# Raw queries and keys in three buffers and loaded three quads ahead, scalings one step sooner, a smaller descriptor scratch, and two small moves around the first expert block

## Chip, core and metric

One core of a Trainium2 chip runs the whole program. The metric is the device time of one execution in microseconds (us), as a median over runs. Engine names are those of the profile: PE (TensorE matmuls), PEld (its weight loads), DVE (VectorE), ACT (ScalarE), POOL (GpSimd), SP (SyncE, which here mainly issues DMAs).

## What is computed

Attention with capped scores for 8 batches, 12 heads, 448 positions and head size 64, and then a mixture of 8 experts with one expert per token over the 3584 resulting rows of 768:

```python
scores = (q @ k.T) / sqrt(64)
scores = cap * tanh(scores / cap)
attn   = softmax(scores)                  # over the last axis
x      = (attn @ v), heads side by side   # [3584, 768]
e      = argmax(x @ w_gate), gate = softmax(x @ w_gate)[e]
out    = gate * (relu(x @ w1[e]) @ w2[e]) # w1: [8, 768, 1024], w2: [8, 1024, 768]
```

All inputs and the output are float32.

## The kernel before, in words

**Attention.** The work is cut into 24 quads (four heads of one batch each, so three quads make a batch), each quad into 7 tiles of 64 keys, and the 168 tiles are taken two at a time in 84 steps. The order on every engine is the order in which the code is written. A step `k` issues, in this order: `scores` and `tanh` of its two tiles (PE, ACT), `expo(k - 1)` (ACT), the products with the values, `values(k)`, of tiles some three steps back (PE), the copies `outp` of a finished quad out of PSUM (DVE), the tasks put down for the places "pe1" and "v0", `adds(k - 2)` (DVE, the sums of the softmax), and the tasks of the places "v1" and "v". A table filled by `at(step, place, function)` says which task stands where.

**Queries.** The raw queries and keys of a quad come by DMA into a tile `qk` (`load(mq, 0)`, the values into `vr` by `load(mq, 1)`), issued from SP. The pool `raw` holds two `qk` tiles, so the load of quad n + 2 waits until PE has read the last scores of quad n. DVE scales the queries in place (`scale_q`, L266), so the scores of a quad wait for its scaling, and the scaling for its DMA. For even quads the scaling stands at place "v0", ahead of `adds`; for odd ones at "v1".

**Routing.** When a batch is finished, its rows go through the gate: `sums`, `rec_v`, `logits`, `log_v` (DVE, its last row is L415, which writes `lr`), then `rec_p` and `log_p` (PE; `log_p`, L427, reads `lr`), `route_v`, `place_p` and so on, spread over the following steps. PE takes `log_p` in its place in the step, ahead of the next step's scores.

**Experts.** Tokens are gathered into blocks of up to 448 rows with indirect DMAs issued from POOL (L742), which have their descriptors in a scratch at the start of each SBUF partition. A first block, number -2, is made from the first three batches and begins beside the end of attention, so that PE has work while the last batch is routed. A block's `up` matmuls (L937) and `down` matmuls (L972) run on weights that ACT and DVE split into a high and a low part (`split_w1`, `split_w2`, L803 and L808). `evac` turns the result out of PSUM (DVE, L1002), and the next block's first `up_ev` (DVE, L950) stands behind it.

**Places the change touches.** `load` and its calls; `raws`, through which `scores`, `scale_q` and `pv` find their tiles; the line that puts `scale_q` into the table; the step loop; the first lines behind that loop (`values(STEPS)`, the first `up_mm(-2, 0)`); the loop over the last `down(-2, f)`, around `rows_x` (which scales, transposes and splits the rows of block 0 in two halves) and `split_w2(0)`; and the construction of the program.

Of the kernel before, what the change touches and what calls it, by code (L numbers as in the profile page):

```python
# [4 lines left out]
F32 = mybir.dt.float32  # L5
# [10 lines left out]
B, H, S, D = 8, 12, 448, 64  # L16
# [7 lines left out]
QB = S // 32  # L24


QN = 11
QR = QB - QN

NQ = NP // 2  # L30
QUADS = B * NQ
KT = S // 64
TILES = QUADS * KT
STEPS = TILES // 2
# [91 lines left out]
def attention_moe(tc, qT, kT, vL, capd, wgL, w1a, w1b, w2a, w2b, cst, cmk, out):  # L126
    nc = tc.nc
    V, A, G, PE = nc.vector, nc.scalar, nc.gpsimd, nc.tensor
    pools = Pools(tc)
# [10 lines left out]
    pb = pools("pb")  # L140
    rpool = pools("rpool", side="right")
    xp = pools("xp", side="right")
    raw = pools("raw", bufs=2, side="right")
    ps_s = pools("ps_s", bufs=2, space=PSUM, side="right")
    ps_o = pools("ps_o", space=PSUM)

# [3 lines left out]

    ids = dpool.tile([(E + 1) * T, 2], I32, name="ids")

    raws = {}
    m = {"xp": xp}
    for i in "hl":
        m["x" + i] = xp.tile([128, KC, LARGE], F32R, name="x" + i)
# [1 line left out]
    def load(mq, part):  # L158

        b, i = divmod(mq, NQ)  # L160
        p = slice(2 * i, 2 * i + 2)
        if part == 0:
            qk = raw.tile([128, 4, S], F32, name="qk")
            raws[mq] = qk[:, 0:2], qk[:, 2:4], pb.tile([128, KT, 2, D], F32, name="vr", bufs=3)
        qr, kr, vr = raws[mq]
        if mq == 0:
            if part == 0:
                nc.sync.dma_start(out=kr[:, :, 0:128], in_=kT[b, :, p, 0:128])
                nc.scalar.dma_start(out=qr[:, 0], in_=qT[b, :, 0])
                nc.sync.dma_start(out=qr[:, 1], in_=qT[b, :, 1])  # L170
                nc.scalar.dma_start(out=capt, in_=capd)
                nc.sync.dma_start(out=kr[:, :, 128:S], in_=kT[b, :, p, 128:S])
            else:
                nc.sync.dma_start(out=vr, in_=vL[b, :, i])
        elif mq == 1:
            if part == 0:
                nc.sync.dma_start(out=kr[:, :, 0:128], in_=kT[b, :, p, 0:128])
                nc.sync.dma_start(out=qr, in_=qT[b, :, p])
            else:
                nc.sync.dma_start(out=kr[:, :, 128:S], in_=kT[b, :, p, 128:S])  # L180
                nc.sync.dma_start(out=vr, in_=vL[b, :, i])
        elif part == 0:
            nc.sync.dma_start(out=kr, in_=kT[b, :, p])
            nc.sync.dma_start(out=qr, in_=qT[b, :, p])
        else:
            nc.sync.dma_start(out=vr, in_=vL[b, :, i])

    capt = att.tile([128, 1], F32, name="capt")
    for part in range(2):
        for g in range(2):  # L190
            load(g, part)
    cs = att.tile([128, C_N], F32, name="cs")
    nc.sync.dma_start(out=cs, in_=cst)
    mk = att.tile([128, 2, 128], BF16, name="mk")
# [1 line left out]
    tri, ones = mk[:, 0], mk[:, 1]  # L196
    wg = att.tile([128, NP, 32], F32, name="wg")
    nc.sync.dma_start(out=wg, in_=wgL)
    w1r = [rpool.tile([128, FC // 2, DM], F32, name=f"w1r{i}") for i in range(2)]
    w2r = [rpool.tile([128, FC // 2, DM], F32, name=f"w2r{i}") for i in range(2)]  # L200
    xg = rpool.tile([128, QB, XR], F32, name="xg")
# [42 lines left out]
    def scores(t):  # L244

        m, g = divmod(t, KT)
        qr, kr, _ = raws[m]
        sp = sps[t] = ps_s.tile([128, 2, 512], F32, name="sp")
        for r in range(2):
            for c in range(2):  # L250
                h, w = slice(64 * r, 64 * r + 64), slice(64 * c, 64 * c + 64)
                PE.matmul(  # L252
                    sp[w, r, 0:S], kr[h, c, 64 * g : 64 * g + 64], qr[h, c, :], start=True, stop=True
                )
# [13 lines left out]
    def expo(k):  # L268
        A.activation(out=pts[k], in_=pts[k], func=AF.Exp, scale=capt)  # L269
# [39 lines left out]

    def pv(t):  # L310
        m, g = divmod(t, KT)
        vr = raws[m][2]
        if g == 0:
            pvs[m] = [ps_o.tile([128, 512], F32, name="po", bufs=2) for _ in range(2)]
        pt = pts[t // 2][:, t % 2]
        for c in range(2):
            for j in range(2):
                r, w = slice(64 * c, 64 * c + 64), slice(64 * j, 64 * j + 64)
                PE.matmul(  # L319
                    pvs[m][c][w, 0:S], vr[r, g, j, :], pt[r, j, :], start=g == 0, stop=g == KT - 1  # L320
                )
# [17 lines left out]
    def strips(ps, operands):  # L339
        own = [(i, i, 0, QN, 0) for i in range(NQ)]  # L340
        rest = [(NQ, 0, QN - 2, QB, 0)] + [(NQ, i, QN, QB, 2 + QR * i) for i in range(1, NQ)]
        runs = [(o, 0) for o in own] + [(rest[0], h) for h in range(2)] + [(o, 1) for o in own]
        runs += [(o, h) for o in rest[1:] for h in range(2)]
        for (g, i, q0, q1, o), h in runs:
            w, x = operands(i, h)
            PE.matmul(
                ps[32 * g : 32 * g + 32, 32 * o : 32 * (o + q1 - q0)],
                w,
                x[:, 32 * q0 : 32 * q1],
                start=h == 0,  # L350
                stop=h == 1,
            )
# [14 lines left out]
    def fill(n=1):  # L367
        while n and filler:
            if next(filler[0], 0) == 0:
                del filler[0]  # L370
            else:
                n -= 1
# [3 lines left out]
    def rec_v(b):  # L376

        st = att.tile([128, QN, 32], F32, name="st")
        V.transpose(out=st, in_=fin[b, "sum"][:, 0 : 32 * QN].rearrange("p (q j) -> p q j", j=32))
        fill()  # L380
        rec = fin[b, "rl"] = att.tile([128, QN, 4], F32, name="rec")
        V.reciprocal(out=rec, in_=st[:, :, 0:4])
# [351 lines left out]
    def width(j):  # L734
        return LARGE if large(j) else SMALL
# [74 lines left out]
    def split_w1(f, e=V, eh=A):  # L810
        high(1, f, eh)
        low(1, f, e)

    def split_w2(f, e=V):
        high(2, f)
        low(2, f, e)
# [97 lines left out]
    def rows_x(j, g):  # L914
        for k in range(KC + 1):
            if k < KC:
                scale_x(j, range(k, k + 1), g)
                trans_x(j, k, g)
            if k > 0:
                split_x(j, k - 1, V, A, g)  # L920
# [5 lines left out]
    def up_mm(j, f, r=None):  # L926
        r = r or slice(0, width(j))
        xh, xl = m["xh"], m["xl"]
        wh, wl = w1s[f]
        if (j, f) not in phs:  # L930
            phs[j, f] = m["ps_h"].tile([128, 512], F32, name="ph")[:, 0 : width(j)]
        ph = phs[j, f][:, r]
        i = 0
        for k in range(KC):
            c = slice(128 * k, 128 * k + 128)
            for w, x in ((wh, xh), (wh, xl), (wl, xh)):
                PE.matmul(ph, w[:, c], x[:, k, r], start=i == 0, stop=i == 3 * KC - 1)  # L937
                i += 1
# [101 lines left out]
    def at(step, when, f, *a):  # L1040
        tasks.setdefault((step, when), []).append((f, a))
# [5 lines left out]
    for b in range(B - 1):  # L1047

        n = (KT * (b * NQ + NQ) - 1) // 2
# [20 lines left out]
    for i in range(QUADS):  # L1070
        if i % NQ != NQ - 1:
            n = (KT * (i + 1) - 1) // 2
# [2 lines left out]

    at(0, "v0", scale_q, 1)
    for i in range(2, QUADS):
        at((KT * (i - 1) - 1) // 2 + 2, "v1" if i % 2 else "v0", scale_q, i)
    n_first = (KT * B_FIRST * NQ - 1) // 2 + 11
    at(0, "v", constants)  # L1080
    at(n_first, "v", first_block)
# [30 lines left out]
    def values(k):  # L1112
        nonlocal held
        last = None
        ready = held + [2 * k - 6, 2 * k - 5]
        held = [ready.pop()] if ready[-2] % KT == KT - 1 else []
        for t in ready:
            pv(t)
            if t % KT == KT - 1:
                last = t // KT  # L1120
        return last

    for k in range(STEPS):
        for n in range(QUADS - 2):
            if k == (KT * (n + 1) - 1) // 2 + 1:
                load(n + 2, 0)
                load(n + 2, 1)
        for t in (2 * k, 2 * k + 1):
            scores(t)
            tanh(t)  # L1130
        do(k, "act")
        if k >= 1:
            expo(k - 1)
        if k >= 3:
            last = values(k)
            if last is not None:
                outp(last)
        do(k, "pe1")
        do(k, "v0")
        if k >= 2:  # L1140
            adds(k - 2)
        do(k, "v1")
        do(k, "v")
        if k == STEPS - 3:
            room()
            split_w1(1, G, G)
# [3 lines left out]
    m["ps_h"] = pools("ps_h", bufs=2, space=PSUM, side="right", **tw)  # L1150
    m["ps_z"] = pools("ps_z", space=PSUM, side="right", **tw)
    expo(STEPS - 1)
    up_mm(-2, 0)
    high(1, 2)
    low(1, 2, G)
    assert values(STEPS) is None
    adds(STEPS - 2)
    do(STEPS, "pe1")
    do(STEPS, "v")
# [87 lines left out]
    for f in range(3, FC):  # L1247
        down(-2, f)
        if f == 3:
            for i in range(6):  # L1250
                split_w1(i)
        elif f == 4:
            rows_x(0, slice(0, QB // 2))
        elif f == 5:
            rows_x(0, slice(QB // 2, QB))
    load_w(1, 0, [1])
    split_w2(0)
    evac(-2)
    pools.close("ps_z", "ps_o")
    m["ps_y"] = pools("ps_y", space=PSUM, **tw)  # L1260
# [108 lines left out]
    with tc.If(more > 0):  # L1369
        for i, name in ((0, "large"), (1, "small")):  # L1370
            cols = range(0, NL) if i == 0 else range(NL, NL + NS)
            cols = [c for c in cols if c not in ORDER]
            n = value(
                tab["nbi"][0:1, i : i + 1], (NL, NS)[i], f"the {name} blocks that hold a token, at most that many"
            )
# [69 lines left out]
```

## Time and profile before

| | us |
|---|---|
| median of 3 runs (812.73 to 814.4) | 813.7 |
| the profiled execution | 813.48 |
| its span, first to last instruction | 811.5 |

| engine | busy us | share of the span |
|---|---|---|
| PE | 781.0 | 96% |
| DVE | 551.3 | 68% |
| ACT | 449.2 | 55% |
| POOL | 407.5 | 50% |

The table is read with the stages in mind: attention fills the first 310 us, in which ACT and PE are both nearly full; from some 390 us to the end PE alone is full with the expert blocks. A busy share over the whole span mixes the two. The profiled execution's time is 2.0 us more than its span.

### The profile page before, as it was taken

To read this page: it belongs to the slowest core of one execution; us is meant where nothing else is said; L and a number is where in the kernel's file an instruction comes from. 1 tells how busy PE (TensorE), PEld (TensorE's weight loads), DVE (VectorE), ACT (ScalarE), POOL (GpSimd) and SP (SyncE) were. 2 spreads that over 40 slices of the span, in tenths; PEclk is the share of its full clock that TensorE was granted. 3 is DMA by queue.
4 is the path that set the end of the run, shared out by engine and by line. 5 is a ranking of instruction groups with operands and counts; after the bars stand their busy time and mean duration, and the time that the engine had idled before them with its cause. 6 is when DMAs were issued, how large, how long until landed. Compare 5 with 4: busy or idle time off the path is not lost.

```text
span 811.5 us, 15070 instructions
## 1 busy us (share of the span) xinstructions
PE 781.0 (96%) x5984; PEld 570.7 (70%) x5984; DVE 551.3 (68%) x908; ACT 449.2 (55%) x534; POOL 407.5 (50%) x400
## 2 busy tenths in 40 slices
PE   8999999999997999999999999999999999999993
PEld 3343434353433435899899999999999999999993
DVE  2778797998896999878549548358357367267720
ACT  7999989989995985343334324224223234234410
POOL 1002230318471367354685784884884883855641
PEclk9999999999998999999999999999999999999998
DMA  6225563478767623493541133543510253354111
GB/s 235 97 110 171 123 190 108 134 229 226 217 137 255 176 77 71 78 344 111 180 158 35 47 105 146 210 141 108 208 55 25 71 199 113 135 195 180 44 62 46
DMA packets 37102, 112.62 MB, mean 139 GB/s; under 512 B 8609, under 2 KB 15699, under 8 KB 34464
## 3 DMA queue, kind: packets, MB, share of 16 engines
q0 software_dynamic: 18528, 63.93, 24.7%
q1 hardware_dynamic: 18208, 47.43, 18.3%
q8 instruction: 49, 0.80, 0.4%
q10 hardware_dynamic: 288, 0.23, 0.1%
q14 instruction: 29, 0.24, 0.1%
HBM read 101.69 MB, written 22.85 MB: 153 GB/s over the span
## 4 chain that ended last, share of the span: by engine, by line
PE 50%; issue 3%; DVE 2%; POOL 1%; DMA 1%; ACT 0%; POOLq 0%; DVEq 0%
PE ph L937 24%; PE y L972 21%; PE y L980 4%; POOL xg L742 1%; DMA xg<-xd,xi 1%; DVE ys L1002 1%; DVE xt L898 0%; DVE xl L906 0%; DVE xg L887 0%; DVE hb L950 0%; DVE w20l L808 0%; POOL ids L513 0%; ACT w20h L803 0%; DVE w16l L808 0%; ACT w16h L803 0%
## 5 line engine op out<-in xcount | busy, mean ns | idle before, releaser
L949 ACT ACTIVATE hb<-ph 128x448 fp32r<-128x448 f32 (+1 forms) x69 | 35.0, 508 | 262.0 <-PE ph L937 262.0
L742 POOL DMA_INDIRECT xg<-xd,xi x114 | 139.7, 1226 | 37.5 <-issue 27.8
L950 DVE SCALAR_TENSOR_TENSOR hb<-ph,hb 128x448 fp32r<-128x448 f32 (+1 forms) x69 | 39.4, 572 | 168.9 <-ACT hb L949 168.9
L262 ACT ACTIVATE pt<-sp 128x896 f32<-128x896 f32 x161 | 140.2, 935 | 24.7 <-PE po L319 15.8
L252 PE MATMUL sp<-qk 64*64 64x448 f32 x1344 | 148.1, 554 | 5.3 <-ACT pt L262 5.2
L269 ACT ACTIVATE pt<-pt,capt 128x1792 f32<-128x1792 f32 x84 | 152.5, 1817 | 0.0
L319 PE MATMUL po<-pt,vr 64*64 64x448 f32 x1344 | 142.9, 540 | 0.0
L752 POOL DMA_INDIRECT out<-ys,xi x98 | 106.0, 1082 | 27.3 <-issue 27.0
L319 PEld LDWEIGHTS po<-pt,vr 64*64 64x64 f32 x1344 | 53.9, 134 | 74.3 <-issue 68.7
L252 PEld LDWEIGHTS sp<-qk 64*64 64x64 f32 x1344 | 43.5, 132 | 83.3 <-ACT pt L262 58.5
L274 DVE TENSOR_TENSOR acc<-acc,pt 128x1792 f32<-128x1792 f32 (+1 forms) x36 | 62.4, 1734 | 8.5 <-ACT pt L269 8.4
L937 PE MATMUL ph<-xh,qk 128*128 128x448 f32 (+2 forms) x228 | 60.5, 340 | 0.0
L482 POOL DMA_DIRECT2D xd<-w2r x12 | 8.4, 708 | 102.2 <-DVE df L455 67.3
L274 DVE TENSOR_TENSOR acc<-pt 128x896 f32<-128x896 f32 (+1 forms) x36 | 51.5, 1437 | 10.6 <-ACT pt L269 10.4
L513 POOL DMA_INDIRECT ids<-tokg,slots x32 | 44.5, 1391 | 27.7 <-DVE slots L507 18.5
L905 ACT CAST xh<-xt 128x448 fp32r<-128x448 f32 (+2 forms) x54 | 25.8, 490 | 34.5 <-DVE xt L898 34.5
L742 POOL DMA_INDIRECT w1r<-in_w1b,widx x7 | 10.5, 1494 | 66.8 <-DVE w17l L808 66.8
L937 PEld LDWEIGHTS ph<-xh,qk 128*128 128x128 f32 x228 | 40.7, 188 | 3.5 <-issue 0.7
L937 PE MATMUL ph<-xl,qk 128*128 128x448 f32 (+2 forms) x114 | 38.6, 339 | 0.0
L326 DVE COPY ot<-po 128x448 f32<-128x448 f32 x48 | 27.3, 610 | 9.6 <-PE po L319 9.5
L898 DVE STREAM_TRANSPOSE xt<-xg 128x448 f32<-128x448 f32 (+2 forms) x60 | 32.5, 550 | 1.4
L482 POOL DMA_DIRECT2D xd<-yt x16 | 10.5, 661 | 41.5 <-DVE mx L453 41.4
(368 smaller groups left out, 1800.4 us busy)
## 6 DMA issues: line engine op xcount, KB each, us to landing
vr<-in_vL SPq DMA_DIRECT2D x24, 448.0 KB, 5.9
qk<-in_qT SPq DMA_DIRECT2D x23, 448.0 KB, 5.4
qk<-in_kT SPq DMA_DIRECT2D x22, 448.0 KB, 4.3
xd<-yt POOLq DMA_DIRECT2D x16, 346.5 KB, 5.0
xd<-w2r POOLq DMA_DIRECT2D x12, 346.5 KB, 5.6
w1r<-in_w1a SPq DMA_DIRECT2D x8, 384.0 KB, 6.9
w1r<-in_w1b SPq DMA_DIRECT2D x8, 384.0 KB, 7.6
w2r<-in_w2b SPq DMA_DIRECT2D x8, 384.0 KB, 5.9
```

Of the source, the lines that this page charges most:

```text
L252: PE.matmul(sp[w, r, 0:S], kr[h, c, 64 * g : 64 * g + 64], qr[h, c, :], start=True, stop=True)
L262: A.activation(out=pts[t // 2][:, t % 2], in_=sps.pop(t)[:, :, 0:S], func=AF.Tanh, scale=scale)
L269: A.activation(out=pts[k], in_=pts[k], func=AF.Exp, scale=capt)
L274: V.tensor_tensor(out=o, in0=a, in1=b, op=ALU.add)
L319: PE.matmul(pvs[m][c][w, 0:S], vr[r, g, j, :], pt[r, j, :], start=g == 0, stop=g == KT - 1)
L513: i = G.indirect_dma_start(out=ids, out_offset=bass.IndirectOffsetOnAxis(ap=slots[0:p, c : c + 1].bitcast(U32), axis=0), in_=tokg[0:p, c, ...
L742: G.indirect_dma_start(out=dst, out_offset=None, in_=src, in_offset=bass.IndirectOffsetOnAxis(ap=idx.bitcast(U32), axis=0), bounds_check=b ...
L752: i = G.indirect_dma_start(out=dst, out_offset=bass.IndirectOffsetOnAxis(ap=idx.bitcast(U32), axis=0), in_=src, in_offset=None, bounds_che ...
L937: PE.matmul(ph, w[:, c], x[:, k, r], start=i == 0, stop=i == 3 * KC - 1)
L949: A.activation(out=hh, in_=ph, func=AF.Relu)
L950: V.scalar_tensor_tensor(out=hl, in0=ph, scalar=0.0, in1=hh, op0=ALU.max, op1=ALU.subtract)
L972: PE.matmul(y[k][:, 0:LARGE], w[:, c], h, start=f == 0 and i == 0, stop=f == FC - 1 and i == 2)
```

## The change

`raw` gets a third buffer. `load(2, 0)` is issued before the loop, and the step that used to load queries and keys of quad n + 2 and then its values now loads the values of quad n + 2 and then queries and keys of quad n + 3. Values get a table of their own (`vrs`). All scalings from quad 2 on stand one step sooner, at place "v1". The descriptor scratch is set to 4096 bytes per partition; without the argument it is 16384. `values(STEPS)` moves ahead of the first `up_mm(-2, 0)`. The split of the first `down` chunk of block 0, `split_w2(0)`, moves from behind the last `down(-2, f)` to between the two halves of `rows_x`.

```diff
+RING = 4096
...
-    raw = pools("raw", bufs=2, side="right")
+    raw = pools("raw", bufs=3, side="right")
...
-    raws = {}
+    raws, vrs = {}, {}
...
-            raws[mq] = qk[:, 0:2], qk[:, 2:4], pb.tile([128, KT, 2, D], F32, name="vr", bufs=3)
-        qr, kr, vr = raws[mq]
+            raws[mq] = qk[:, 0:2], qk[:, 2:4]
+        qr, kr = raws[mq]
+        if part == 1:
+            vr = vrs[mq] = pb.tile([128, KT, 2, D], F32, name="vr", bufs=3)
...
     nc.sync.dma_start(out=wg, in_=wgL)
+    load(2, 0)
...
     for i in range(2, QUADS):
-        at((KT * (i - 1) - 1) // 2 + 2, "v1" if i % 2 else "v0", scale_q, i)
+        at((KT * (i - 1) - 1) // 2 + 1, "v1", scale_q, i)
...
             if k == (KT * (n + 1) - 1) // 2 + 1:
-                load(n + 2, 0)
                 load(n + 2, 1)
+                if n + 3 < QUADS:
+                    load(n + 3, 0)
...
     expo(STEPS - 1)
+    assert values(STEPS) is None
     up_mm(-2, 0)
     high(1, 2)
     low(1, 2, G)
-    assert values(STEPS) is None
...
         elif f == 4:
             rows_x(0, slice(0, QB // 2))
+            split_w2(0)
         elif f == 5:
             rows_x(0, slice(QB // 2, QB))
     load_w(1, 0, [1])
-    split_w2(0)
...
-    nc = bacc.Bacc("TRN2", target_bir_lowering=False, num_devices=1)
+    nc = bacc.Bacc(
+        "TRN2", target_bir_lowering=False, num_devices=1, dynamic_dma_scratch_size=RING
+    )
```

How the instructions move is seen best in the order on three engines. On SP, at the start of the program (`cs`, `mk`, `wg` are constants, `ids` a table that is filled once, `qk` holds keys from `in_kT` and queries from `in_qT`, `vr` values), before:

```order
L198 DMA wg<-in_wgL 128x192
L237 DMA ids<-w1r_114 128x504
L183 DMA qk<-in_kT 128x896
L184 DMA qk<-in_qT 128x896
L186 DMA vr<-in_vL 128x896
```

and with the change:

```order
L200 DMA wg<-in_wgL 128x192
L186 DMA qk<-in_kT 128x896
L187 DMA qk<-in_qT 128x896
L240 DMA ids<-w1r_117 128x504
L189 DMA vr<-in_vL 128x896
```

The queries and keys of quad 2 stand ahead of the fill of `ids`, and from there on each triple is values, keys, queries, with the keys and queries one quad further on.

On DVE, where batch 5 is routed (`acc` and `p` are softmax sums, `yt` and `xt` transposes, the four rows from `lt` to the second `lr` are `log_v`), before:

```order
L274 TENSOR_TENSOR acc<-acc,pt 128x1792
L337 STREAM_TRANSPOSE yt<-ot 128x14x32
L898 STREAM_TRANSPOSE xt<-xg 128x448
L266 TENSOR_SCALAR qk<-qk,qsc 128x896
L274 TENSOR_TENSOR p_2556<-acc 128x896
L274 TENSOR_TENSOR p_2556<-p_2556,pt 128x896
L406 STREAM_TRANSPOSE lt<-ms 128x352
L409 TENSOR_TENSOR lt<-lt,rec 128x352
L413 TENSOR_REDUCE lr<-lt 96x88
L415 TENSOR_REDUCE lr<-lt 32x24
L326 COPY ot<-po 128x448 x2
```

and with the change:

```order
L277 TENSOR_TENSOR acc<-acc,pt 128x1792
L269 TENSOR_SCALAR qk<-qk,qsc 128x896
L340 STREAM_TRANSPOSE yt<-ot 128x14x32
L901 STREAM_TRANSPOSE xt<-xg 128x448
L277 TENSOR_TENSOR p_2559<-acc 128x896
L277 TENSOR_TENSOR p_2559<-p_2559,pt 128x896
L409 STREAM_TRANSPOSE lt<-ms 128x352
L412 TENSOR_TENSOR lt<-lt,rec 128x352
L416 TENSOR_REDUCE lr<-lt 96x88
L418 TENSOR_REDUCE lr<-lt 32x24
L329 COPY ot<-po 128x448 x2
```

The scaling stays ahead of the two sums and of `log_v`, two rows further up.

On DVE, at the end of block -2 (`xl` is the low part of block 0's rows, `w20l` the low part of its first `down` chunk, `ys` the rows of block -2 turned out of PSUM, `hb` the first `up_ev` of block 0), before:

```order
L898 STREAM_TRANSPOSE xt<-xg 128x224
L906 TENSOR_TENSOR xl<-xt,xh 128x224 x2
L808 TENSOR_TENSOR w20l<-w2r_116,w20h 128x768
L1002 STREAM_TRANSPOSE ys<-z_3665 128x14x32
L1002 STREAM_TRANSPOSE ys<-z_3666 128x14x32
L1002 STREAM_TRANSPOSE ys<-po 128x14x32 x2
L1002 STREAM_TRANSPOSE ys<-ms 128x14x32 x2
L950 SCALAR_TENSOR_TENSOR hb<-ph,hb 128x448 x2
```

and with the change, at the turn from the first half of block 0's rows to the second (`sc`, `xg` and the last `xt` are of the second half):

```order
L901 STREAM_TRANSPOSE xt<-xg 128x224
L909 TENSOR_TENSOR xl<-xt,xh 128x224 x2
L811 TENSOR_TENSOR w20l<-w2r_119,w20h 128x768
L881 TENSOR_TENSOR sc<-xg,idt 128x42
L890 TENSOR_TENSOR xg<-xg,sc 128x7x32
```

The row `w20l` has left the place between the last `xl` and the first `ys`, which now follow each other, and stands some twenty rows further up; its counterpart on ACT, the cast that writes `w20h`, moves in the same way from behind twelve casts of `xh` to between the sixth and the seventh.

## Rows read from the trace of the kernel before

**Rows 1.** The page's first line, and part 4's shares of the chain.

```profile
span 811.5 us, 15070 instructions
...
PE 50%; issue 3%; DVE 2%; POOL 1%; DMA 1%; ACT 0%; POOLq 0%; DVEq 0%
```

**Rows 2.** Windows: length, busy (count) of PE, PEld, DVE, ACT, POOL; PEclk, DMA share, GB/s.

```profile
190.00:200.00 10.00, 9.99 (x107) 3.43 (x107) 8.05 (x9) 10.00 (x11) 8.48 (x7) 1.00 0.91 289
250.00:260.00 10.00, 4.63 (x68) 1.97 (x68) 9.37 (x13) 2.32 (x2) 0.00 (x0) 0.72 0.72 284
256.00:257.00 1.00, 1.00 (x16) 0.44 (x15) 0.97 (x3) 0.00 (x0) 0.00 (x0) 0.50 0.87 328
380.00:390.00 10.00, 8.54 (x62) 8.01 (x62) 9.22 (x17) 4.42 (x8) 0.97 (x1) 1.00 0.06 23
```

**Rows 3.** Waits from 240 to 263 us: total us, times, longest.

```profile
ACT pt L262 <- PE po L319: 8.6, 1, 8.6
...
DVE qk L266 <- DMA qk<-in_qT: 4.9, 1, 4.9
```

**Rows 4.** Timeline around 250 us: start, length, engine, row [idle before, releaser].

```profile
250.38 0.69 DVE L266 TENSOR_SCALAR qk<-qk,qsc 128x896 f32<-128x896 f32 x1 [4.87 <-DMA qk<-in_qT]
250.51 1.81 ACT L269 ACTIVATE pt<-pt,capt 128x1792 f32<-128x1792 f32 x1
...
255.82 0.34 PE L427 MATMUL ms<-lr,cs 128*32 128x32 f32 x8 [5.37 <-DVE lr L415]
...
262.52 1.79 ACT L269 ACTIVATE pt<-pt,capt 128x1792 f32<-128x1792 f32 x1
```

**Rows 5.** Timeline around 100 us, the same place in batch 1.

```profile
96.76 0.69 DVE L266 TENSOR_SCALAR qk<-qk,qsc 128x896 f32<-128x896 f32 x1 [2.91 <-PE sp L252]
...
100.20 1.80 ACT L269 ACTIVATE pt<-pt,capt 128x1792 f32<-128x1792 f32 x1
...
102.20 0.27 PE L427 MATMUL ms<-lr,cs 128*32 128x32 f32 x8 [2.07 <-DVE lr L415]
...
106.56 1.79 ACT L269 ACTIVATE pt<-pt,capt 128x1792 f32<-128x1792 f32 x1
```

**Rows 6.** Timeline around 180 us, ACT's exponentials at the same place in batch 3.

```profile
176.41 1.81 ACT L269 ACTIVATE pt<-pt,capt 128x1792 f32<-128x1792 f32 x1
...
180.86 1.79 ACT L269 ACTIVATE pt<-pt,capt 128x1792 f32<-128x1792 f32 x1
```

**Rows 7.** Timeline of DVE (256 to 300 us, all its waits) and of ACT behind it.

```profile
264.34 2.30 DVE L274 TENSOR_TENSOR acc<-acc,pt 128x1792 f32<-128x1792 f32 x1 [1.44 <-ACT pt L269]
...
284.21 1.31 DVE L274 TENSOR_TENSOR acc<-pt 128x896 f32<-128x896 f32 x1 [0.25 <-ACT pt L269]
...
293.80 1.16 DVE L326 COPY ot<-po 128x448 f32<-128x448 f32 x2 [0.21 <-PE po L319]
...
300.15 1.73 ACT L262 ACTIVATE pt<-sp 128x896 f32<-128x896 f32 x2 [1.87 <-DVE acc L274]
```

**Rows 8.** Timeline of the turn from attention to block -2, PE and DVE.

```profile
307.91 0.44 PE L937 MATMUL ph<-xh,w10h 128*128 128x448 f32 x1 [0.76 <-ACT pt L262]
...
311.87 0.47 PE L937 MATMUL ph<-xl,w10h 128*128 128x448 f32 x1 [0.47 <-POOL xl L906]
...
323.31 0.55 DVE L379 STREAM_TRANSPOSE st<-ms 128x352 f32<-128x352 f32 x1 [0.79 <-PE ms L346]
```

**Rows 9.** Timeline of the turn from block -2 to block 0, DVE and PE.

```profile
374.74 0.20 DVE L878 TENSOR_TENSOR sc<-xg,idt 128x42 f32<-128x42 f32 x1 [2.11 <-DMA xg<-xd,xi]
...
381.81 0.96 DVE L808 TENSOR_TENSOR w20l<-w2r,w20h 128x768 fp32r<-128x768 f32 x1 [0.34 <-ACT w20h L803]
...
386.55 0.48 PE L972 MATMUL y<-hb,w20h 128*128 128x448 f32 x1 [1.46 <-DVE hb L950]
```

**Rows 10.** POOL's gathers of block 0: length min/median/max in ns, first and last start; landing.

```profile
L742 POOL DMA_INDIRECT xg<-xd,xi x14: 998/1112/1517, 352.3 to 371.8; - x14
...
DMA to landing us min/median/max: 2.6/2.9/6.0
```

More of the change, by code (lines that the diff above doesn't have):

```diff
@@ L188, in attention_moe @@
     capt = att.tile([128, 1], F32, name="capt")
-    for part in range(2):
-        for g in range(2):
-            load(g, part)
+    for part, g in ((0, 0), (0, 1), (1, 0), (1, 1)):
+        load(g, part)
     cs = att.tile([128, C_N], F32, name="cs")
@@ L246, in scores @@
         m, g = divmod(t, KT)
-        qr, kr, _ = raws[m]
+        qr, kr = raws[m]
         sp = sps[t] = ps_s.tile([128, 2, 512], F32, name="sp")
@@ L311, in pv @@
         m, g = divmod(t, KT)
-        vr = raws[m][2]
+        vr = vrs[m]
         if g == 0:
```

## The prediction

> **What bounds the kernel now.** I read the chain of waits first: of a span of 811.5 us it gives PE half and no other engine more than 2% [rows 1]. That half is the expert blocks behind 386.55 us, where block 0's `down` begins [rows 9]; this change touches nothing there, so that stretch keeps its length and can only start earlier. What is to be won lies ahead of it. The windows of 10 us come next. In an undisturbed stretch of attention ACT is busy for 10.0 us of 10 and PE for 9.99 [rows 2]: both are full, and no other engine's edit helps there. Two windows stand out: at 250 us PE has 4.63 us, ACT 2.32 us and a granted clock of 0.72, and at 380 us PE has 8.54 us [rows 2]. So I asked who waits in the first one. ACT waited 8.6 us for PE, and DVE 4.9 us for the DMA of raw queries [rows 3]. The timeline puts these in one line: DVE stands 4.87 us at the scaling of quad 20; the rows behind it, up to `lr`, are late by that; PE has taken `log_p` in its place, stands 5.37 us, and with it the scores for ACT [rows 4]. The same place in batch 1 has a gap of 2.91 us at the scaling and 2.07 us at `log_p` [rows 5]. (The trace names a PE row as releaser there, but quad 8's buffer had long been loaded into and PE does not write it; I read that, too, as the load.) Batch 3 has no such stall, and gives the price of this place without one: from one exponential to the next 4.45 us [rows 6], against 6.36 us in batch 1 [rows 5] and 12.01 us in batch 5 [rows 4].
>
> **The change, part by part.**
>
> *Loads a quad ahead, scalings a step sooner.* A quad is 3.5 steps. Between the exponentials of batch 1 and batch 3 at 100.20 and 176.41 us [rows 5, 6] lie 21 steps, so a step is 3.63 us on the mean and a quad 12.7 us. A load that starts in the same step as now, but for a quad later, has that much more time; the step that the scalings give back takes some 3.6 us of it. The remaining 9 us exceed the 4.87 and 2.91 us that were missing. Both waits go.
>
> Batch 1: PE's 2.07 us at `log_p` go if `lr` is early enough, and it is, since DVE gets 2.91 us. By the intervals the gain is 6.36 - 4.45 = 1.91 us. I take 2.0 us (bounds 1.9 and 2.1).
>
> Batch 5: DVE has `lr` 4.87 us sooner, so `log_p` goes at 255.82 - 4.87 = 250.95 us, while PE gets there at 255.82 - 5.37 = 250.45 us: 0.5 us of the stall stays. The scaling itself moves up two rows in the same unbroken run of DVE work, so it relieves nothing there. By PE and ACT the interval becomes 4.45 + 0.5 = 4.95 us, a gain of 12.01 - 4.95 = 7.1 us. That is more than the 4.87 us, because the stall also cost clock: half the clock, 1.2 GHz, was granted to the matmuls behind it, as the window of 1 us at 256 us shows [rows 2], and without 5.37 us of idle PE I see nothing that lowers it. But DVE has to follow. After the stall it waits 1.44, 0.25 and 0.21 us up to 300 us [rows 7] and is otherwise full, so at 300 us, where ACT already waits 1.87 us for DVE [rows 7], DVE can have won at most 4.87 + 1.44 + 0.25 + 0.21 = 6.77 us. I take the smaller, 6.8 us. Lower bound: if DVE keeps all it won behind it busy with POOL's competing work, the 4.87 us alone. Upper bound: the whole excess, 12.01 - 4.45 = 7.6 us.
>
> *What is queued behind moved rows.* On SP the load of queries and keys still waits for PE, as now; the values' load goes ahead of it and waits for nothing that is late, and the weight loads behind stay behind the same wait. `load(2, 0)` at the start puts two DMAs of 448 KB ahead of the fill of `ids`, which nobody reads for many steps, and behind the loads that the first steps need. I cost this at nothing; it could cost at most the time of its transfer on a shared queue, a few us at the start, if the first values were pushed back, but they stand ahead of it in the queue. Odd scalings now stand ahead of a routing row or two on DVE, 0.69 us each [rows 5]; PE's `place_p` is a step later and hides it.
>
> *`values(STEPS)` first.* At the turn PE waits 0.76 us for ACT to free PSUM and 0.47 us for POOL's last `xl` [rows 8]. Sixteen matmuls of values whose exponentials are long done now stand in the first gap and push `up_mm(-2, 0)` back past the second. The other values, whose exponentials come last, still stand behind the 18 `up` matmuls, as now, so I see no new wait there. PE gains 1.23 us; DVE, next in line at the last batch's routing, waited 0.79 us for PE there [rows 8] and gains no more than that and a little. I take 1.0 us (bounds 0 and 1.2).
>
> *The first down chunk.* DVE stands 2.11 us between the two halves of block 0's rows [rows 9]. ACT's cast and DVE's 0.96 us fit into it; the raw weights' loads were issued well before the gathers that this gap waits for. At the old place it took 0.34 + 0.96 us, less some 0.1 us of overlap, on the chain to `hb`, for which PE stands 1.46 us [rows 9]. Gain 1.2 us (bounds 0 and 1.46). About 0.3 us of the gap remains.
>
> *Scratch of 4096 bytes.* No row shows the scratch, so I bound it. Below: nothing, as no row of POOL names it as a releaser. Above: POOL waits at each gather until the one before has landed. Block 0's 14 gathers start from 352.3 to 371.8 us, 1.5 us apart, and land in 2.9 us at the median [rows 10]; one after the other they would take 1.0 + 2.9 = 3.9 us each. So two to four are in flight at once (6.0 us at the longest landing). I take nothing, because so few in flight are nearer to an empty scratch than to a full one. The Trainium skill has a rule that speaks against the edit: its page Debugging Trainium Hangs (section Descriptor Overflow) names too many descriptors for a carveout of 16 KiB per partition as a cause of hangs. By its page DMA: Bandwidth & Descriptors (Terms, and The descriptor swizzle) a descriptor is 16 bytes and a transfer to 128 partitions makes 9 per engine and side; 4096 bytes would then hold an estimated 28 such transfers, well over those in flight here.
>
> **Sum.** 2.0 + 6.8 + 1.0 + 1.2 + 0 = 11.0 us off the profiled execution's 813.48 us (its span and 2.0 us around it), which is 0.2 us under the median of 813.7 us. Against the median that is 802.7 us. With all lower bounds, 1.9 + 4.9 + 0 + 0 = 6.8 us: 806.9 us. With all upper ones, 2.1 + 7.6 + 1.2 + 1.5 = 12.4 us: 801.3 us. What attention wins shifts the rest as a whole: the last batch's routing, the gathers and block -2 all start from it, and PE, at 10 us of 10 between them, keeps its work.
>
> **The rivals.**
>
> *DVE takes the stall's place.* It was 9.37 us busy even in the stalled window [rows 2]. If it falls behind before 300 us, ACT's wait of 1.87 us [rows 7] grows and most of the clock's part and of the turn's 1.0 us are lost: 2.0 + 4.9 + 1.2 = 8.1 us, 805.6 us. Against it: nearly all its rows are the same and it needs only to run on.
>
> *Slower: the scratch.* If gathers go one at a time, the 13 intervals of block 0's gathers grow from 1.5 to 3.9 us, 31 us on the chain to block 0: 802.7 + 31 = 834 us, and more if later blocks lose too. It decides from 11.0 / 13 = 0.85 us of added wait per gather on. For it speaks only that the scratch is a quarter; against it, the two to four in flight.
>
> *The change doesn't do what it says.* The loads could be late for a reason that moves along with them: DMA engines busy with weights and stored rows, whoever is first in the queue. Then DVE stands at a later scaling and only the turn's terms remain, 2.2 us: 811.5 us; without those, 813.7 us. Against it: the gap needed is 4.87 us and the lead grows by 9.
>
> *More than forecast.* Small waits of DVE on loads or of PE on DVE elsewhere go as well, worth 1 to 2 us: 801 us.
>
> **Chances.** Forecast (801.3 to 804) 0.6; DVE in its place (804 to 807) 0.2; more than forecast 0.08; only the turn, or nothing, 0.07, half of it within 0.2%; scratch 0.05. The range 800.3 to 806.9 leaves out about 2 in 10 with what I may have missed. By 0.2% (1.6 us, about what a measurement of this kernel can tell from no change): faster 0.91, same 0.04, slower 0.05.
>
> **What would show it.** Right: no DMA among the releasers of `scale_q` after the first steps; the exponentials' intervals at batches 1 and 5 at 4.4 to 5.0 us; a granted clock of 1.00 in every window of attention; PE's gaps at the turn and ahead of block 0's second `down` matmul gone or under 0.4 us; gathers still 1.5 us apart. Wrong: a new long wait of ACT on DVE around 290 us; POOL rows of 2 us and more; the first window with less of PE than now.

## Result and the profile after

The changed kernel takes 805.32 us (median of 4, 804.61 to 805.92) against 814.05 us for the kernel before beside it (812.73 to 814.64): a ratio of 0.9892 with an interval of 0.9876 to 0.9908, 8.7 us less. The profiled execution has 804.61 us and a span of 802.7 us, 8.8 us shorter than that of before. The forecast was 802.7 us in a range of 800.3 to 806.9 us, so its gain of 11.0 us was 2.3 us too large. The trace shows that two larger misses of opposite sign make most of this, one at the turn and one at the program's end.

The attention stage first, as in [rows 2]. The windows of the changed kernel (busy time and count of PE, PEld, DVE, ACT and POOL, then granted clock, DMA share and GB/s):

```profile
190.00:200.00 10.00, 10.00 (x114) 3.84 (x110) 7.40 (x8) 10.00 (x10) 8.48 (x6) 1.00 0.83 200
240.00:250.00 10.00, 9.29 (x144) 4.32 (x140) 9.78 (x13) 9.18 (x9) 3.20 (x2) 1.00 1.02 240
250.00:260.00 10.00, 10.00 (x113) 3.81 (x106) 9.80 (x17) 8.40 (x10) 4.24 (x4) 1.00 0.90 298
...
300.00:310.00 10.00, 7.24 (x39) 5.05 (x40) 9.81 (x16) 4.91 (x5) 5.87 (x5) 0.83 0.30 63
380.00:390.00 10.00, 10.00 (x53) 9.10 (x52) 5.27 (x9) 4.33 (x7) 4.91 (x6) 1.00 0.33 120
```

The hole at 250 us is gone (PE 4.63 us before, 10.00 now, clock 1.00), and so is the one at 380 us. A new one stands at 300 us: PE 7.24 us at a clock of 0.83. Batch 5 in the timeline of the changed kernel, which answers to [rows 4]:

```profile
248.57 1.81 ACT L272 ACTIVATE pt<-pt,capt 128x1792 f32<-128x1792 f32 x1
...
249.22 0.27 PE L430 MATMUL ms<-lr,cs 128*32 128x32 f32 x8 [0.71 <-DVE lr L418]
...
253.59 1.79 ACT L272 ACTIVATE pt<-pt,capt 128x1792 f32<-128x1792 f32 x1
...
253.94 0.68 DVE L269 TENSOR_SCALAR qk<-qk,qsc 128x896 f32<-128x896 f32 x1
```

The interval of the exponentials is 5.02 us, for 12.01 before, and PE's wait for `lr` 0.71 us, for 5.37. Batch 1, the place of [rows 5]:

```profile
100.20 0.28 PE L430 MATMUL ms<-lr,cs 128*32 128x32 f32 x8
...
100.43 1.81 ACT L272 ACTIVATE pt<-pt,capt 128x1792 f32<-128x1792 f32 x1
...
104.57 1.79 ACT L272 ACTIVATE pt<-pt,capt 128x1792 f32<-128x1792 f32 x1
```

The interval is 4.14 us, for 6.36, with no wait of PE. Behind batch 5 something is given back. In the timeline these rows of PE and ACT name DVE as releaser, and the last row is the last pair of exponentials:

```profile
262.53 1.88 PE L322 MATMUL po<-pt,vr 64*64 64x448 f32 x14 [1.10 <-DVE ot L329]
...
266.19 1.73 ACT L265 ACTIVATE pt<-sp 128x896 f32<-128x896 f32 x2 [0.81 <-DVE acc L277]
...
292.41 1.73 ACT L265 ACTIVATE pt<-sp 128x896 f32<-128x896 f32 x2 [1.88 <-DVE acc L277]
...
300.69 3.50 ACT L272 ACTIVATE pt<-pt,capt 128x1792 f32<-128x1792 f32 x2
```

In ACT's timeline of before, that pair is this row:

```profile
308.43 3.50 ACT L269 ACTIVATE pt<-pt,capt 128x1792 f32<-128x1792 f32 x2
```

It now starts at 300.69 us: attention has won 7.7 us. The turn, which answers to [rows 8], in the timeline of PE and DVE:

```profile
298.48 0.93 PE L322 MATMUL po<-pt,vr 64*64 64x448 f32 x8
...
302.12 1.12 DVE L329 COPY ot<-po 128x448 f32<-128x448 f32 x2
...
302.76 4.19 PE L322 MATMUL po<-pt,vr 64*64 64x448 f32 x24 [3.34 <-DVE ot L329]
...
306.87 0.47 PE L940 MATMUL ph<-xh,w10h 128*128 128x448 f32 x1
...
310.73 3.24 PE L322 MATMUL po<-pt,vr 64*64 64x448 f32 x32
...
319.26 0.55 DVE L382 STREAM_TRANSPOSE st<-ms 128x352 f32<-128x352 f32 x1 [3.05 <-PE ms L349]
```

PE stands 3.34 us for `ot` (DVE's `outp(22)`), and the 24 matmuls behind it take 4.19 us, while 32 of the same kind at full clock take 3.24. Two windows in them show the clock at its lower level (1.2 GHz) for most of the time, 0.58 from 302 to 304 us and then:

```profile
304.00:306.00 2.00, 2.00 (x16) 1.21 (x12) 1.97 (x4) 0.91 (x2) 1.06 (x2) 0.57 0.00 0
```

The `st` of the last batch comes 4.05 us sooner than in [rows 8], where the last pair of exponentials came 7.74 us sooner: the turn has lost 3.7 us. Then block 0, as in [rows 9] and [rows 10], first the timeline, then the source line of the gathers:

```profile
369.13 0.96 DVE L811 TENSOR_TENSOR w20l<-w2r,w20h 128x768 fp32r<-128x768 f32 x1 [0.34 <-ACT w20h L806]
370.43 0.20 DVE L881 TENSOR_TENSOR sc<-xg,idt 128x42 f32<-128x42 f32 x1 [0.33 <-DMA xg<-xd,xi]
...
380.65 0.75 PE L975 MATMUL y<-hb,w20h 128*128 128x448 f32 x2
```

```profile
L745 POOL DMA_INDIRECT xg<-xd,xi x14: 997/1017/1526, 348.3 to 367.7; - x14
```

DVE's gap between the halves is 0.33 us, PE's wait of 1.46 us is gone, and the gathers start 1.5 us apart as before. The first gather is 4.1 us sooner (352.3 to 348.3). At the last scatter, in POOL's timeline of before and then of the changed kernel, it is 5.7 us:

```profile
800.59 0.97 POOL L752 DMA_INDIRECT out<-ys,oi  x1 [2.09 <-DVE ys L1012]
```

```profile
794.93 0.97 POOL L755 DMA_INDIRECT out<-ys,oi  x1 [2.09 <-DVE ys L1015]
```

From there to the end of the span are 10.9 us before (811.5 - 800.59) and 7.8 us now (802.7 - 794.93). So 3.1 us come from behind the last work of any engine. The queue rows of the program's last source line show what stands there: the longest of POOL's DRAINs, 4893 ns before and 2362 ns now (minimum/median/maximum in ns, then the first and the last start in us). It is the first of the three: begun at 805.8 us it ends at 810.7 us, and the last begins at 811.2 us.

```profile
L1441 POOLq DRAIN  x3: 40/107/4893, 805.8 to 811.2; - x3
```

```profile
L1447 POOLq DRAIN  x3: 40/107/2362, 799.5 to 802.5; - x3
```

So the span's gain is 7.7 (attention) - 3.7 (turn) + 1.6 (block 0) + 3.1 (end) = 8.8 us with the rounding.

### The profile page after: what moved, and what is told of

Same layout as the page of the kernel before. It is cut to its first block, busy times and chain, and to the rows that moved or that the text cites. A ratio compares the mean times of both kernels' runs of the same rounds, so it can differ in the third digit from the quotient of the medians.

```text
span 802.7 us, 15069 instructions
## 1 busy us (share of the span) xinstructions
PE 780.4 (97%) x5984; PEld 571.4 (71%) x5984; DVE 551.7 (69%) x908; ACT 449.4 (56%) x534; POOL 411.4 (51%) x400
## 4 chain that ended last, share of the span: by engine, by line
PE 81%; ACT 7%; DVE 6%; issue 2%; POOL 2%; DMA 1%; POOLq 0%; DVEq 0%; ACTq 0%
PE ph L940 29%; PE y L975 22%; PE po L322 10%; PE sp L255 10%; PE y L983 4%; ACT pt L265 4%; ACT pt L272 3%; PE ms L349 2%; DVE acc L277 2%; POOL xg L745 1%; PE po L975 1%; PE z L975 1%; PE ms L975 1%; DMA xg<-xd,xi 1%; DVE ot L329 1%
## 5 line engine op out<-in xcount | busy, mean ns | idle before, releaser
L277 DVE TENSOR_TENSOR acc<-pt 128x896 f32<-128x896 f32 (+1 forms) x36 | 51.4, 1428 | 11.0 <-ACT pt L272 10.7
L890 DVE TENSOR_TENSOR xg<-xg,sc 128x448 f32<-128x448 f32 (+2 forms) x60 | 30.2, 551 | 0.3
```

The costliest lines, as they stand in the source:

```text
L277: V.tensor_tensor(out=o, in0=a, in1=b, op=ALU.add)
```

## Experiments

Every ratio is to the kernel before on the same chip, with its 95% interval. It is not the quotient of the two medians; a gain given behind it is worked out from the ratio where the two differ (e3 0.9 us for 1.3 by the medians, e6 2.9 for 3.8, e9 8.0 for 7.5). e1 to e4 ran together, so did e5, e6, e9 and e10, and so did e7, e8 and the repeat of e1.

### e1: the values back behind the `up` matmuls

```
-    assert values(STEPS) is None
     up_mm(-2, 0)
     high(1, 2)
     low(1, 2, G)
+    assert values(STEPS) is None
```

> The changed kernel with `values(STEPS)` back behind `low(1, 2, G)`. Theory A (the first value matmul of quad 23 waits for DVE's `outp` of quad 22 to empty PSUM `po`, and the PE wait of 3.3 us and the low clock behind it are the cost of the move): PE's wait on `ot` goes, the window of 300 to 310 us gets its clock of 1.00 back, `sums` of the last batch comes 3.5 to 4 us sooner, and the kernel takes 3.7 us less than the changed one, about 801.6 us. Theory B (DVE, not PE, sets the turn, and would have lost the 3.7 us in any order): the wait goes but `sums` stays where it is, and the time stays within 1 us of 805.3 us.

Measured: 800.91 us against 814.32, ratio 0.9837 (0.9825 to 0.9850), below the changed kernel's interval. The turn in the timeline of e1:

```profile
300.16 0.44 PE L940 MATMUL ph<-xh,w10h 128*128 128x448 f32 x1 [0.76 <-ACT pt L265]
...
304.09 0.47 PE L940 MATMUL ph<-xl,w10h 128*128 128x448 f32 x1 [0.45 <-POOL xl L909]
...
304.70 5.49 PE L322 MATMUL po<-pt,vr 64*64 64x448 f32 x56
...
315.50 0.55 DVE L382 STREAM_TRANSPOSE st<-ms 128x352 f32<-128x352 f32 x1 [0.72 <-PE ms L349]
```

And its window at the turn:

```profile
300.00:310.00 10.00, 9.39 (x74) 5.27 (x74) 9.82 (x16) 5.67 (x6) 5.88 (x5) 1.00 0.31 65
```

The two old waits are back, the 3.34 us are gone, the clock is 1.00, and `st` comes 3.76 us sooner. Theory A holds, theory B falls: DVE is busy for 9.8 us of 10 in both orders, and yet the order decides. (The two intervals come from two sets of runs; the profiled spans, 802.7 us of the changed kernel and 798.9 us of e1, differ by 3.8 us.)

A second set of runs, beside e8:

> The kernel of e1 again, beside e8 on one chip: a ratio to before of 0.9837 within 0.0015, if the differences between e1, e5, e8 and e10 can be read at all.

801.20 us against 813.72, ratio 0.9844 (0.9831 to 0.9858). Differences under 1 us are at the edge of what these intervals tell, and are read from the traces below.

### e2 and e7: the scratch alone

```
-    nc = bacc.Bacc("TRN2", target_bir_lowering=False, num_devices=1)
+    nc = bacc.Bacc("TRN2", target_bir_lowering=False, num_devices=1, dynamic_dma_scratch_size=4096)
```

> The kernel before with only the descriptor scratch of 4096 bytes. Theory A (the end of the program drains POOL's descriptor scratch, and that DRAIN of 4.9 us is shorter with a smaller one): the last DRAIN on POOL's queue takes 2.4 us, everything ahead of it is unchanged, and the time is 2.5 us less, 811.5 us. Theory B (the end differs from execution to execution, or follows from the loads): the DRAIN stays at 4.9 us and the time within 0.5 us of before. Theory C (a smaller scratch makes gathers wait): block 0's gathers start more than 1.6 us apart and the time rises.

Measured: 810.20 us against 814.32, ratio 0.9952 (0.9939 to 0.9966), 2.8 to 5.0 us less. e7 is the same edit with 8192:

> The kernel before with a scratch of 8192 bytes, between the 16384 of before and the 4096 of e2. Theory A (the last DRAIN on POOL's queue goes by the size of the scratch, 4.89 us and 2.36 us at the two ends, 0.21 us per 1024 bytes): the DRAIN takes 3.2 us, and the time falls by 1.7 us. Theory B (there are two states, with and without some leftover in the scratch): the DRAIN takes 4.9 or 2.4 us.

Measured: 812.11 us against 813.72, ratio 0.9983 (0.9972 to 0.9994), 0.5 to 2.3 us less. The DRAIN of e7, in the same view as above; that of e2 has the changed kernel's 2362 ns:

```profile
L1441 POOLq DRAIN  x3: 40/107/3342, 805.4 to 809.3; - x3
```

4893, 3342 and 2362 ns at 16384, 8192 and 4096 bytes: theory A, but for the word "last", since this DRAIN is the first of three. The whole stretch from the last scatter to the end follows: 10.7 to 11.0 us in the five profiles at 16384 bytes (before, e3, e4, e6, e9), 8.9 us in e7, and 7.6 to 7.9 us in the seven at 4096. So the scratch is worth 3.1 us, of which the DRAIN's own 2.5 us are located; the other 0.6 us lie between the last scatter and the DRAIN, and what makes them is open. e2's median gain of 4.1 us is above 3.1, but its interval reaches to 2.8. Theory C falls: block 0's gathers start 1.5 us apart in e2, too.

### e3: the first down chunk alone

```
             rows_x(0, slice(0, QB // 2))
+            split_w2(0)
 ...
     load_w(1, 0, [1])
-    split_w2(0)
```

> The kernel before with only `split_w2(0)` moved between the halves of block 0's rows. Theory A (the prediction's term): DVE's gap of 2.1 us between the halves shrinks to about 0.3 us by the cast and the subtraction in it, PE's wait of 1.46 us at block 0's second `down` matmul goes, and the time falls by 1.2 us. Theory B (the chain from the last gathered rows to the last block of -2 sets the end, and DVE's 0.96 us were hidden): no change, or a loss of up to 1 us if the second half of the rows is held up.

Measured: 813.04 us against 814.32, ratio 0.9989 (0.9979 to 0.9999): 0.9 us, with 0.1 to 1.7. In the timeline of e3 the cast's rest and the subtraction stand in the gap, which shrinks from 2.11 to 0.31 us:

```profile
373.69 0.96 DVE L808 TENSOR_TENSOR w20l<-w2r,w20h 128x768 fp32r<-128x768 f32 x1 [0.34 <-ACT w20h L803]
374.96 0.20 DVE L878 TENSOR_TENSOR sc<-xg,idt 128x42 f32<-128x42 f32 x1 [0.31 <-DMA xg<-xd,xi]
```

The view of waits from 340 to 400 us lists none of PE's. The first gather is 0.3 us later than in the profile of before (352.64 for 352.32) and the last scatter 1.06 us sooner (799.53 for 800.59), so the edit gives 1.4 us by the traces: theory A. The other profiles bear it out: from the first gather to the last scatter are 447.9 to 449.3 us in the six without the edit and 446.5 to 446.9 us in the seven with it (e3 among them).

### e4: the values' move alone

```
+    assert values(STEPS) is None
     up_mm(-2, 0)
     high(1, 2)
     low(1, 2, G)
-    assert values(STEPS) is None
```

> The kernel before with only `values(STEPS)` moved ahead of `up_mm(-2, 0)`. Theory A (PSUM `po` of quad 22 is emptied late by DVE in the kernel before as well): PE waits 3 to 4 us for `ot` at the first value matmul of quad 23, and the time rises by 3.5 to 5 us, to 817 to 819 us. Theory B (the prediction's term, the wait in the changed kernel comes from its other parts): PE's waits of 0.76 and 0.47 us go and the time falls by 1.0 us.

Measured: 819.32 us against 814.32, ratio 1.0061 (1.0048 to 1.0074): 5 us more. The wait in the timeline of e4 is there without any other part of the change:

```profile
311.16 3.00 PE L319 MATMUL po<-pt,vr 64*64 64x448 f32 x24 [3.36 <-DVE ot L326]
```

Theory A. In this profiled execution (816.62 us, mean clock 0.990) the 24 matmuls take 3.00 us, for 4.19 in the changed kernel; its windows of 1 us from 311 to 316 us have a clock of 1.00. From the last pair of exponentials to `st` are 17.4 us there, 14.9 before and 18.6 in the changed kernel: the wait alone costs 2.5 us, and with the clock's fall it is 3.7. A PE wait of nearly the same length (3.36 and 3.34 us) was followed by a fall of the clock in one program and by none in this execution; why is open. The other four executions took 818.6 to 819.4 us at mean clocks of 0.986 to 0.988. That they lost the clock at this place is likely, but no trace of them shows it.

### e5: the loads without the sooner scalings

On e1:

```
-        at((KT * (i - 1) - 1) // 2 + 1, "v1", scale_q, i)
+        at((KT * (i - 1) - 1) // 2 + 2, "v1" if i % 2 else "v0", scale_q, i)
```

> The kernel of e1 with the scalings at their old steps: three buffers and the loads a quad ahead, but no sooner scaling. Theory A (the loads alone end DVE's waits, and the scaling's step moves nothing): no DMA among the releasers of `scale_q`, the intervals of batches 1 and 5 as in the changed kernel within 0.3 us, and the time within 0.5 us of e1, a ratio of 0.983 to 0.985. Theory B (the sooner scaling has its own part, because DVE's rows come in another order): batch 5 loses 1 us or more against e1.

Measured: 801.92 us against 814.11, ratio 0.9843 (0.9827 to 0.9860), not to be told from e1. `scale_q` has no DMA wait after the start. The difference that the trace shows lies in batch 5, where PE waits twice as long for `lr` as in the changed kernel (0.71 us):

```profile
250.02 0.27 PE L430 MATMUL ms<-lr,cs 128*32 128x32 f32 x8 [1.51 <-DVE lr L418]
```

So the loads alone, a quad ahead in three buffers, end the waits (theory A). But the interval of batch 5 is 5.86 us, for 5.02 in the changed kernel, more than the 0.3 us that theory A allowed and less than theory B's 1 us, and the last pair of exponentials is 0.8 us later than in e1's second profile. Of theory B there are thus 0.8 us in the trace and nothing that the times resolve. The place where they arise is DVE's work ahead of that `lr`. At its old step the scaling stands behind the transpose `xt`, on which POOL's `xl` waits, and the two adds that follow run beside it in DVE's timeline of e5:

```profile
243.49 0.65 DVE L269 TENSOR_SCALAR qk<-qk,qsc 128x896 f32<-128x896 f32 x1
244.05 1.45 DVE L277 TENSOR_TENSOR p<-acc 128x896 f32<-128x896 f32 x1
245.60 1.86 DVE L277 TENSOR_TENSOR p<-p,pt 128x896 f32<-128x896 f32 x1
```

In the changed kernel the scaling stands ahead of `xt` (242.18 us), and the same adds take 1.05 and 1.26 us. That POOL's rows beside them are the reason is likely, but no run took them away.

### e6: the sooner scalings without the loads

The same line of `scale_q`, the other way round, in the kernel before.

> The kernel before with only the scalings a step sooner, on two buffers. Loads start there 7 to 12 us ahead of their scaling and land after 4 to 7 us at the median; a step sooner leaves 3.5 to 9 us. Theory A (a sooner scaling on the old loads lengthens DVE's waits): `scale_q` waits for loads in about half of the quads, 1 to 3 us each, the two long stalls grow by up to 3.6 us, and the time rises by 3 to 15 us. Theory B (DVE has enough slack, or the stall only changes its place): the time stays within 2 us of before.

Measured: 817.91 us against 814.11, ratio 1.0035 (1.0023 to 1.0048): 2.9 us more (1.9 to 3.9), the low end of theory A. The source line of `scale_q` in e6 lists what DVE was idle for ahead of it (us, times):

```profile
  DMA qk<-in_qT: 9.1, 6
  PE po L319: 6.0, 1
  PE sp L252: 2.0, 1
```

Before it was 7.9 us at two places for the DMA, with the program's start, and the 2.9 us of [rows 5]. The waits come at seven places after the start, fewer than expected, and of the 6.3 us by which their sum grows more than half is hidden; the one in batch 5 grows from 4.87 to 5.95 us. (The releaser named there is a matmul; as in [rows 5], I read it as the load.) So the two halves of this edit are not alike: the third buffer with the loads a quad ahead brings the gain, and the sooner scaling is harmless only with it.

### e9: the late loads left, DVE's row taken away

```
-        scale = qsc if t < KT else 1.0
+        scale = qsc if t // KT in (0, 8, 20) else 1.0
 ...
     for i in range(2, QUADS):
+        if i in (0, 8, 20):
+            continue
```

> The kernel before, but quads 8 and 20 are not scaled by DVE: their tanh takes the scale, as quad 0's does, so DVE has nothing to wait for there while the loads stay as late as they were. 14 tanh get 0.08 us longer (1.00 against 0.93 us in quad 0 and 1). Theory A (the late load costs only because DVE, in order, stands at the scaling with the routing rows behind it): batches 1 and 5 go as in the changed kernel, 2.2 and 6 to 7 us, less up to 1.1 us for ACT: 5.5 to 8 us less than before. Theory B (the load is late for PE as well, or DMA is the bound there): PE waits for the load of quad 20 instead, and the gain stays under 3 us.

Measured: 806.62 us against 814.11, ratio 0.9902 (0.9885 to 0.9918), 8.0 us less with two scalings fewer on DVE and their 14 tanh longer. Batch 5 in the timeline of e9:

```profile
249.00 1.81 ACT L269 ACTIVATE pt<-pt,capt 128x1792 f32<-128x1792 f32 x1
...
249.29 0.27 PE L427 MATMUL ms<-lr,cs 128*32 128x32 f32 x8 [0.35 <-DVE lr L415]
...
252.04 1.91 ACT L262 ACTIVATE pt<-sp,qsc 128x896 f32<-128x896 f32 x2 [1.23 <-PE po L319]
...
253.84 1.79 ACT L269 ACTIVATE pt<-pt,capt 128x1792 f32<-128x1792 f32 x1
```

The interval is 4.84 us and PE does not wait for the load. Theory A: the load was never late for its user, PE. It cost what it did because DVE, which works in order, stood at a scaling that was due two steps later, with `lr` behind it.

### e8 and e10: DVE relieved behind batch 5

Both start from e1. e10 scales quads 20 to 23 in their tanh, as e9; e8 on POOL:

```
-        V.tensor_scalar_mul(qr, qr, qsc)
+        (G if mq >= 20 else V).tensor_scalar_mul(qr, qr, qsc)
```

> The kernel of e1 with quads 20 to 23 scaled in their tanh: DVE loses 4 rows of 0.68 us in the stretch from 240 to 290 us, ACT gets 28 tanh 0.08 us longer, 2.2 us in all. Theory A (DVE, 98% busy from 240 to 310 us, is the limit behind the removed stall and gave 1.2 us back at two steps, and ACT's wait of 1.9 us near 292 us is its doing): those give-backs and waits shrink by about 2.7 us, and the time falls by 1 to 2.5 us against e1, a ratio of 0.981 to 0.983. Theory B (ACT is as full there): ACT's 2.2 us eat it, and the time stays within 0.7 us of e1.

Measured: 801.45 us against 814.11, ratio 0.9842 (0.9825 to 0.9859): no gain over e1 that the times show, theory B. In its trace 0.8 us of the give-back are won at one step and 0.6 us at three others, but the other nine steps of these quads are 0.19 us longer each on ACT, and that eats it.

> The kernel of e1 with quads 20 to 23 scaled by POOL instead of DVE (as e10, but at no cost to ACT). Theory A (behind the removed stall DVE is the limit): DVE's give-back of 1.0 us near 264 us and ACT's wait of 1.9 us near 292 us shrink, and the time falls by 0.7 to 1.5 us against e1, a ratio of 0.982 to 0.983. Theory B (POOL's rows of 2 us and more beside DVE's make DVE slower, or POOL, in order behind rows that wait for DVE, scales late): the give-backs stay, or PE waits for the scaled queries, and the time is that of e1 or up to 5 us more.

Measured: 800.36 us (800.12 to 801.50) against 813.72, ratio 0.9837 (0.9823 to 0.9851), beside 801.20 us for e1 on the same chip. The row of DVE's give-back in the timeline of e8, 1.10 us in the changed kernel:

```profile
262.18 1.88 PE L322 MATMUL po<-pt,vr 64*64 64x448 f32 x14 [0.45 <-DVE ot L329]
...
265.83 1.73 ACT L265 ACTIVATE pt<-sp 128x896 f32<-128x896 f32 x2 [0.21 <-DVE acc L277]
```

ACT's 0.81 us there became 0.21. Its last pair of exponentials is 0.9 us sooner than in e1's second profile, 0.3 us of which were there at 83 us already, long before the edit. The times alone don't separate e8 from e1, so theory A has the trace for it and no more; ACT's 1.9 us near 292 us stayed. Both e1 and e8 beat the kernel before and the changed one.

## Why the prediction was right, and where not

**What bounds attention** was right. The stall was DVE's wait for the load with `lr` behind it (e9), and the third buffer takes it away (e5). Batch 1 was forecast at 2.0 us and gave 2.2 at its interval; small shifts up to 240 us make that 1.95 (the exponential of 239.73 us comes at 237.78).

**Batch 5** was forecast at 7.1 us by PE and ACT, and cut to 6.8 by DVE. The interval gave 7.0 us, and two later steps took 1.2 back. So the mechanism was right, DVE follows and decides (e9 for the stall; for the give-backs the releasers and e8's trace), and the term was 1.0 us too large: 5.8 us. From DVE's first `lr` row of batch 5 to `outp(22)` are 55.56 us before (254.32 to 309.88) and 54.41 now (247.71 to 302.12): 1.15 us of its waits were won where the sum had counted all 1.9. Of the rest, 0.4 us stayed waits, and its rows there took 0.35 us longer in sum (53.03 us busy for 52.68). "It relieves nothing there", of the scaling's new place, was not quite right either: e5's trace gives it 0.8 us in batch 5.

**The values at the turn** is the step that failed: "Sixteen matmuls of values whose exponentials are long done now stand in the first gap", and "I see no new wait there". It was forecast to win 1.0 us, with 0 as the lower bound; it cost 3.7 us. The prediction asked whether the exponentials were there, and they were. It did not ask for the matmuls' destination: they begin quad 23, whose PSUM `po` has two buffers, both taken by quad 22 until DVE copies them out. The code had held the tile back behind `up_mm(-2, 0)`, in whose time DVE came to that copy. The trace of before had the row, in DVE's timeline, 2 us behind the first `up` matmul of [rows 8]:

```profile
309.88 1.11 DVE L326 COPY ot<-po 128x448 f32<-128x448 f32 x2
```

PE would have come to the values at 307.15 us (307.91 - 0.76). The row is two copies, one for each buffer, and PE needs the first; in the changed kernel it went on 0.64 us after their start (302.76 for 302.12), which here is 310.52 us. That is a wait of 3.4 us ahead of work that had hidden it, and e4, the same order with nothing else changed, has 3.36. Two more points were off: 24 matmuls moved, not sixteen, and the idle PE then lost clock, which the prediction had charged for the stall in batch 5 but not looked for here (e4 gives 2.5 us for the wait alone).

**The first down chunk** was right: 1.2 us forecast, 1.4 by e3's trace and 1.6 in the changed kernel (5.66 us at the last scatter less 4.06 at the first gather). The row at 386.55 us in [rows 9] is block 0's second `down` matmul, and not where its `down` begins.

**The scratch** was forecast at nothing, with "nothing" as the lower bound as well. The gathers did stay 1.5 us apart, and the argument on the transfers in flight held. But a gain was excluded by looking at POOL's rows alone. The 3.1 us lie in the stretch behind the last scatter's start, 10.9 us of the span in which nothing else is computed, and which the prediction never opened.

**The signs.** Right: no DMA among the releasers of `scale_q` after the start; a clock of 1.00 in every window of 10 us up to 300 us; block 0's wait gone; as much of PE in the first window as before (8.34 us for 8.35). Near: intervals of 4.14 and 5.02 us, just outside the 4.4 to 5.0 forecast. POOL rows of 2 us and more are there (11 up to 310 us), but before there were 13, so that sign tells nothing. Right, too: ACT's wait for DVE near the end of attention 1.88 us, for 1.87 before, so the rival in which DVE takes the stall's place did not come in the form it was given. Wrong: PE's gap at the turn, and the clock of 0.83 there. That the time fell inside the range, and as near as it did, is in part luck, for the misses partly cancel: 4.7 us too much at the turn (+1.0 forecast, -3.7 measured) and 1.0 in batch 5, 3.1 too little at the end and 0.4 in block 0.

## What to carry to other kernels

When a block of matmuls is moved forward, ask for three things before costing it at nothing: its operands, the buffer it writes into, and the row of the other engine that frees that buffer. An engine that waits in order for data which nobody needs yet makes everything behind it late; another buffer, or giving its row to an engine that is at that place anyway (e9), was worth about the same here (the last pair of exponentials starts at 301.11 us in e9, 300.68 and 301.02 in e1's two profiles). Read the stretch between the last working row and the end of the span, too: it can hold microseconds that a setting of the program changes.

## What the runs showed of the hardware

The long DRAIN on POOL's queue at the program's end goes by the size of the descriptor scratch: 4.89, 3.34 and 2.36 us at 16384, 8192 and 4096 bytes. The Trainium skill, on its page VectorE: DVE Perf Modes (section The DRAIN you can't avoid), tells of DRAINs of about 12 ns that every program has on all engines at its begin and end. The trace agrees by length for the other engines at the program's last line in the kernel before (7 to 17 ns), but not for POOL (40, 107 and 4893 ns); whether the page means these rows or others, no run here shows.

A scaling of 128x896 elements that takes DVE 0.68 us took POOL 2.5 to 2.8 us in e8:

```profile
247.53 2.78 POOL L269 TENSOR_SCALAR qk<-qk,qsc 128x896 f32<-128x896 f32 x1
```

The Trainium skill, on its page GPSIMD Engine Reference (section Engine selection), calls POOL roughly line-rate for work with one input. Here it was about four times as slow as DVE, with DVE at work beside it; in e8 it lay where POOL had idle time.
